# Winograd convolution with batch norm and SiLU: the first chunk's taps loaded in quarters between the x loads, and two matmuls on zeros ahead of the x tiles 2 to 14

## The chip, the cores and the metric

The kernel runs on one core of a Trainium2 chip. Time is device microseconds of that core; the median of three runs before the change is 193.27 us (192.41, 193.27 and 194.06). The engines are called by the profile's names: PE multiplies matrices (PEld loads its stationary operand), DVE and ACT are the vector and scalar engines, POOL is GpSimd, and SP issues nearly all transfers. Transfers run on 16 DMA engines, which share every load between them.

## The reference

The kernel computes a convolution over the sequence with three taps, then a batch norm with given statistics, then SiLU. The inputs are bfloat16.

```python
B, S, C = 2, 2048, 1024          # w is [3, C, C]
xp = jnp.pad(x, ((0, 0), (1, 1), (0, 0)))
y = sum(jnp.einsum('bsc,cd->bsd', xp[:, k:k + S, :], w[k]) for k in range(3))
y = (y - mean) * (g / jnp.sqrt(var + 1e-5)) + b
return jax.nn.silu(y)
```

## The kernel before, in words

The convolution is done by Winograd's method: six outputs of the sequence are made from eight inputs by eight products in place of eighteen. So there are three kinds of work.

**The x transform.** A batch's 2048 rows are cut into 17 windows of 126 rows (128 with the overlap), the last with 33. In this document w0 to w16 are the windows of batch 0 and w0' to w16' those of batch 1. `load_window` (L205 to L216) issues a window's load on SP: 128 rows of 2 KB, 256 KB in all. `transform` (L218 to L241) multiplies pieces of the window by a constant matrix `Rm` into PSUM (L225, 168 columns a matmul), and then one copy on ACT or DVE (L239, L241), chosen by a running cost, brings the group to `T_sb`. For batch 0 a window is two groups of four matmuls; each group has two PSUM banks, and the eight banks go round, so that a group reuses the banks of the group four before.

**The weight transform.** The output channels come in eight chunks of 128. A chunk's three taps are 256 KB each and are loaded as 1024 pieces of 256 bytes (`load_chunk`, L89). POOL makes six combinations of the taps from them, `uch` (`pair_sum` L163, `scale_weights` L149, `pair_tap` L173); the two other products use the raw taps 0 and 2. For chunk 0 POOL's order is: the sum of taps 0 and 2 (L163), tap 2 scaled, a second sum, tap 0 scaled, a third sum, then the first `uch` (L173), tap 1 scaled, and the five further `uch`.

**The units.** A unit is one chunk and one batch: eight products of eight matmuls each (`mms`, L250, 342 columns), and the output transform on ACT and DVE (L291, L298). The first unit (chunk 0, batch 0) takes product 7 first, which needs only the raw tap 2, and then 1, 3, 2, 4, 5, 0 and 6. Its matmuls are interleaved with the transform of batch 1: after each group of it a share of the first unit is run. From the second unit on there are only units, 64 matmuls each.

The order of each engine is the order in which the program is written (`manual_schedule`). On SP that means that a load that must wait holds back all that follow. There are two such waits. An x window's buffer is one of ten, so that a load waits until PE is done with the window ten before. And every load gets one of eight completion semaphores in turn, shared with the four parameter loads of the ACT queue: a load is issued only when the load eight before it has landed on all 16 engines.

The loop around the change, in the version before:

```python
for wi in range(NWIN):
    window = load_window(xpool, 0, wi)
    if wi in (3, 5, 13):
        load_chunk(0, {3: 0, 5: 2, 13: 1}[wi])
    for h in range(2):
        transform(0, wi, window, 4 * h, 4, (2 * wi + h) % 4 * 2, 2)
    if wi == 7: ...        # POOL: the sums of taps 0 and 2, with the scaling of taps 2 and 0
    if wi == 13: ...       # POOL: the six uch, with the scaling of tap 1
```

Seven matmuls on zeros (L203, 512 columns) stand ahead of everything on PE.

Of the kernel before, what the change touches and what calls it, by code (L numbers as in the profile page):

```python
# [32 lines left out]
NJ = 8  # L33
# [4 lines left out]
def kernel(  # L38
# [10 lines left out]
    nc = tc.nc  # L49
    B, S, C = x.shape  # L50
    D = w.shape[2]
    P = 128
    CT = C // P
# [19 lines left out]
    w_all = w.rearrange("k (ct p) d -> p k ct d", p=P)  # L73
    raw, wts, wx = {}, {}, {}
# [9 lines left out]
    def load_weights(dp):  # L84
        open_weights(dp)
        for k in (0, 2, 1):
            nc.sync.dma_start(out=pair_tile[dp][:, k], in_=w_all[:, k, :, dp * 2 * P:(dp + 1) * 2 * P])

    def load_chunk(dc, k):  # L89
        nc.sync.dma_start(out=raw[dc][k], in_=w_all[:, k, :, dc * P:(dc + 1) * P])  # L90

    open_weights(0)

# [15 lines left out]
    warm = consts.tile([P, 512], BF16, name="warm")  # L109
# [16 lines left out]
    for j in (0, 7):  # L126
        for k in range(NJ):
            if BT[j][k] != 0:
                nc.gpsimd.affine_select(
                    out=Rm[:, j, :],  # L130
                    in_=Rm[:, j, :],
# [12 lines left out]
    def scale_weights(dc, taps=(2, 1, 0), on_gpsimd=False):  # L144
        for k in taps:
            f = 2.0 if k == 1 else 4.0
            dst = wx[dc, k] = wtmp.tile([P, CT, P], BF16, name=f"w{k}x")
            if on_gpsimd:
                nc.gpsimd.tensor_scalar(dst, raw[dc][k], f, 0.0, op0=ALU.mult, op1=ALU.add)  # L149
            else:  # L150
                nc.scalar.mul(dst, raw[dc][k], f)

    def open_chunk(dc):
        wts[dc] = upool.tile([P, 6, CT, P], BF16, name="uch")
# [3 lines left out]
    def pair_sum(dc, n, engine=nc.gpsimd):  # L158

        e = outer[dc, n] = wtmp.tile([P, CT, P], FP32, name=("e1", "e2", "eh")[n])  # L160
        a = wx[dc, 0] if n == 2 else raw[dc][0]
        c = wx[dc, 2] if n == 1 else raw[dc][2]
        engine.tensor_tensor(e, a, c, op=ALU.add)  # L163
# [7 lines left out]
    def pair_tap(dc, n, op):  # L171
        odd = wx[dc, 1] if n else raw[dc][1]
        nc.gpsimd.tensor_tensor(wts[dc][:, 2 * n + (op == ALU.subtract)], outer[dc, n], odd, op=op)  # L173
# [14 lines left out]
    def turn_params():  # L188
        nc.tensor.transpose(prmT.rearrange("p q d -> p (q d)"), prm, ident[0:4 * DC, 0:4 * DC])
        nc.vector.tensor_scalar(rstd, prmT[:, 0, :], 1e-5, 1.0, op0=ALU.add, op1=ALU.mult)  # L190
        nc.gpsimd.tensor_tensor(rstd, rstd, mhalf, op=ALU.pow)

    def make_params():
        nc.vector.tensor_tensor(sc, prmT[:, 1, :], rstd, op=ALU.mult)
        nc.vector.tensor_tensor(beta, prmT[:, 2, :], sc, op=ALU.mult)
        nc.vector.tensor_tensor(beta, prmT[:, 3, :], beta, op=ALU.subtract)
        nc.vector.scalar_tensor_tensor(out=sk, in0=prmT[:, 1, :], scalar=C1, in1=rstd, op0=ALU.mult, op1=ALU.mult)
# [7 lines left out]
    def load_window(xpool, bi, wi):  # L205
        ntile = min(WT, NTB - WT * wi)
        t_lo = M_OUT * WT * wi - 1
        t_hi = min(t_lo + M_OUT * ntile + 1, S - 1)
        kk = t_hi - t_lo + 1
        if t_lo < 0:  # L210
            nc.sync.dma_start(out=xw0[1:113, :], in_=x[bi, 0:112, :])
            nc.sync.dma_start(out=xw0[113:kk, :], in_=x[bi, 112:t_hi + 1, :])
            return xw0, kk, ntile
        xw = xpool.tile([P, C], BF16, name="xw")
        nc.sync.dma_start(out=xw[0:kk, :], in_=x[bi, t_lo:t_hi + 1, :])  # L215
        return xw, kk, ntile  # L216

    def transform(bi, wi, window, ct0, n, bk, per):  # L218

        xw, kk, ntile = window  # L220
        width = 512 // per if per != 3 else 168
        banks = ps_all[:, bk * 512:(bk + (n + per - 1) // per) * 512]
        for c in range(n):
            at = (c // per) * 512 + (c % per) * width
            nc.tensor.matmul(  # L225
                banks[:, at:at + NJ * ntile],
                lhsT=xw[0:kk, (ct0 + c) * P:(ct0 + c + 1) * P],
                rhs=Rm[0:kk, :, 0:ntile],
                start=True,
                stop=True,  # L230
            )
        src = banks[:, 0:n * width].rearrange("p (s e) -> p s e", e=width)
        src = src[:, :, 0:NJ * ntile].rearrange("p s (j n) -> p s j n", j=NJ)
        dst = T_sb[bi][:, ct0:ct0 + n, :, WT * wi:WT * wi + ntile]
        cost = {e: f + m * n for e, (f, m) in EVAC.items()}
        eng = min(load, key=lambda e: load[e] + cost[e])
        load[eng] += cost[eng]
        if eng == "act":
            nc.scalar.copy(dst, src)  # L239
        else:  # L240
            nc.vector.tensor_copy(dst, src)  # L241
# [97 lines left out]
    def run(gen, n=None):  # L339
        while n is None or n > 0:  # L340
            if next(gen, run) is run:
                return
            if n is not None:
                n -= 1
# [3 lines left out]
    with tc.tile_pool(name="xwin", bufs=10) as xpool:  # L348
        for wi in range(NWIN):
            window = load_window(xpool, 0, wi)  # L350
            if wi in (3, 5, 13):
                load_chunk(0, {3: 0, 5: 2, 13: 1}[wi])
            for h in range(2):
                transform(0, wi, window, 4 * h, 4, (2 * wi + h) % 4 * 2, 2)
            if wi == 0:
                turn_params()
            if wi == 7:
                open_chunk(0)
                for n, taps in ((0, ()), (1, (2,)), (2, (0,))):
                    scale_weights(0, taps, on_gpsimd=True)  # L360
                    pair_sum(0, n)
            if wi == 13:
                pair_tap(0, 0, ALU.add)
                scale_weights(0, (1,), on_gpsimd=True)
                for n, op in ((1, ALU.add), (0, ALU.subtract), (1, ALU.subtract), (2, ALU.add), (2, ALU.subtract)):
                    pair_tap(0, n, op)
        make_params()
        first = unit(0, 0, 0, NTB, (0, 1, 2, 3), yTs[0], late, seven_first=True)
        load["act"] = load["dve"] = 0.0
        gi, done = 0, 0  # L370
        for wi in range(NWIN):
            window = load_window(xpool, 1, wi)
            if wi == 10:
                for k in (0, 2, 1):
                    load_chunk(1, k)
            for ct0, n in ((0, 3), (3, 3), (6, 2)):
                transform(1, wi, window, ct0, n, 4 + gi % 4, 3)
                gi += 1
                want = 52 * max(gi - 1, 0) // (3 * NWIN - 1)
                run(first, want - done)  # L380
                done = want
        load_weights(1)
        run(first)
# [68 lines left out]
    dc, bi = units[-1]  # L452
# [148 lines left out]
```

## Time and profile before

| what | before |
|---|---|
| median of 3 runs | 193.27 us |
| the profiled execution's own time | 193.53 us |
| its span, first to last instruction | 191.7 us |
| PE busy | 180.0 us (94%) |
| DVE busy | 161.3 us (84%) |
| POOL busy | 148.0 us (77%) |
| ACT busy | 122.6 us (64%) |
| mean granted clock of PE | 0.975 |
| moved by DMA | 31.72 MB |

The profile comes from one execution, and its times are microseconds from the first instruction. The 1.8 us between its span and its own time lie outside the instructions. A row of the timeline has the start, the length, the engine, the line, the operation and the tile (or tiles) that it writes and reads, and in brackets the idle time before it with what ended it. In a table of stretches each row has the busy time (and the number of instructions) of every engine in that stretch, then the clock that the throttle granted to PE (PEclk, 1.00 is full speed), the busy share of the DMA engines and the rate. Beside these views the trace keeps, for every load, sixteen completion counts, one for each DMA engine, with their times.

### The profile page before, as it was taken

The page shows a single profiled execution, that of the slowest core. Times are in us where ns is not written, and L with a number is a line of the kernel's source. Part 1 is how long each engine was busy: PE and PEld are TensorE (multiplying, and loading weights), DVE is VectorE, ACT ScalarE, POOL GpSimd, SP SyncE. Part 2 cuts the span into 40 slices and gives each one's busy share as a digit, 9 for nine tenths or more (in the row PEclk, how much of TensorE's full clock was granted, in tenths as well). Part 3 has the DMA queues.
Part 4 walks back from the last instruction along what each step waited for, and adds up shares of the span by engine and source line. Part 5 has one row for each costly group of instructions (what it writes and reads, how often), then busy time and mean ns, then how long its engine had stood idle before and what let it go on. Part 6 is the DMA issues. An engine that isn't in the chain of part 4 may idle for free.

```text
span 191.7 us, 3904 instructions
## 1 busy us (share of the span) xinstructions
PE 180.0 (94%) x1404; PEld 128.0 (67%) x1404; DVE 161.3 (84%) x347; ACT 122.6 (64%) x201; POOL 148.0 (77%) x89
## 2 busy tenths in 40 slices
PE   7579999999999999999999999999999999999960
PEld 3369688866666666666666666666666666669950
DVE  6557999987999699969996999699969987788981
ACT  3747878888287726873786287638755873635770
POOL 6359999999949996999699969996999699900000
PEclk9966999999999999999999999999999999999996
DMA  4999997990608387999292989783746465566425
GB/s 124 323 369 305 329 292 202 285 221 0 123 0 170 69 184 196 275 142 202 46 192 57 205 228 243 147 180 68 168 81 151 95 143 108 124 120 160 118 66 105
DMA packets 86759, 31.72 MB, mean 165 GB/s; under 512 B 73364, under 2 KB 82580, under 8 KB 86740
## 3 DMA queue, kind: packets, MB, share of 16 engines
q1 hardware_dynamic: 86637, 31.46, 70.1%
q8 instruction: 11, 0.18, 0.4%
q14 instruction: 8, 0.07, 0.1%
q10 hardware_dynamic: 103, 0.02, 0.0%
HBM read 14.82 MB, written 8.39 MB: 121 GB/s over the span
## 4 chain that ended last, share of the span: by engine, by line
PE 84%; DVE 6%; DMA 5%; ACT 2%; SPq 1%; issue 1%; DVEq 0%; ACTq 0%
PE ps_all L250 75%; PE ps_all L225 8%; DMA xw<-in_x_dram 5%; DVE T_sb L241 3%; ACT yT L261 1%; DVE y L487 1%; PE ps_all L465 1%; SPq L215 1%; DVE y L291 0%; SPq L90 0%; DVE d L487 0%; DVE ps_all L487 0%; DVE o_end L568 0%; ACT s L507 0%; ACT m L501 0%
## 5 line engine op out<-in xcount | busy, mean ns | idle before, releaser
L250 PE MATMUL ps_all<-T_sb,uch 128*128 128x342 bf16 (+2 forms) x816 | 123.0, 299 | 0.0
L250 PEld LDWEIGHTS <-uch 128*128 128x128 bf16 x816 | 77.0, 97 | 33.2 <-issue 0.2
L261 ACT ACTIVATE yT<-y,beta,sk 128x684 bf16<-128x684 f32 (+5 forms) x46 | 44.2, 960 | 30.3 <-DVE y L291 29.6
L250 PE MATMUL ps_all<-T_sb,wch 128*128 128x342 bf16 (+2 forms) x272 | 44.0, 300 | 0.2 <-DVE T_sb L241 0.2
L291 DVE SCALAR_TENSOR_TENSOR y<-ps_all,y 128x342 f32<-128x342 f32 x90 | 41.9, 507 | 1.7 <-PE ps_all L250 0.7
L173 POOL TENSOR_TENSOR uch<-e,wch 128x1024 bf16<-128x1024 f32 x16 | 33.8, 2134 | 10.8 <-PE ps_all L250 5.9
L173 POOL TENSOR_TENSOR uch<-e,w1x 128x1024 bf16<-128x1024 f32 x16 | 33.8, 2135 | 0.6
L225 PE MATMUL ps_all<-Rm,xw 128*128 128x168 bf16 (+1 forms) x272 | 31.2, 251 | 3.2 <-DMA xw<-in_x_dram 2.8
L173 POOL TENSOR_TENSOR uch<-eh,w1x 128x1024 bf16<-128x1024 f32 x16 | 33.8, 2132 | 0.6
L250 PEld LDWEIGHTS <-wch 128*128 128x128 bf16 x272 | 25.6, 97 | 11.5 <-DVE T_sb L241 0.4
L239 ACT CAST T_sb<-ps_all 128x672 bf16<-128x672 f32 (+5 forms) x45 | 26.3, 606 | 9.4 <-PE ps_all L225 8.3
L298 ACT COPY m<-ps_all 128x342 f32<-128x342 f32 x45 | 19.9, 442 | 19.0 <-PE ps_all L250 18.3
L241 DVE CAST T_sb<-ps_all 128x672 bf16<-128x672 f32 (+3 forms) x40 | 26.3, 698 | 5.6 <-PE ps_all L225 5.2
L225 PEld LDWEIGHTS <-xw 128*128 128x128 bf16 (+1 forms) x272 | 24.6, 106 | 8.5 <-DMA xw<-in_x_dram 3.5
L291 DVE SCALAR_TENSOR_TENSOR y<-ps_all,d 128x342 f32<-128x342 f32 x45 | 20.3, 507 | 0.5
L163 POOL TENSOR_TENSOR e<-wch,w2x 128x1024 f32<-128x1024 bf16 x8 | 17.0, 2130 | 0.2
L163 POOL TENSOR_TENSOR eh<-w0x,wch 128x1024 f32<-128x1024 bf16 x8 | 17.1, 2132 | 0.1
L291 DVE SCALAR_TENSOR_TENSOR y<-ps_all,s 128x342 f32<-128x342 f32 x30 | 14.0, 508 | 3.2 <-ACT s L298 3.2
L291 DVE SCALAR_TENSOR_TENSOR d<-m,ps_all 128x342 f32<-128x342 f32 x15 | 7.6, 507 | 9.3 <-ACT s L298 9.3
L291 DVE SCALAR_TENSOR_TENSOR ps_all<-m,ps_all 128x342 f32<-128x342 f32 x30 | 15.3, 509 | 0.0
L169 DVE TENSOR_REDUCE e<-wch 128x1024 f32<-128x2048 bf16 x6 | 13.7, 2277 | 0.0
L298 ACT COPY s<-ps_all 128x342 f32<-128x342 f32 x30 | 13.1, 438 | 0.0
(65 smaller groups left out, 83.4 us busy)
## 6 DMA issues: line engine op xcount, KB each, us to landing
xw<-in_x_dram SPq DMA_DIRECT2D x30, 256.0 KB
out_dram<-o_sb SPq DMA_DIRECT2D x30, 192.0 KB
wch<-in_w_dram SPq DMA_DIRECT2D x9, 512.0 KB
out_dram<-o_sb SPq DMA_DIRECT2D x15, 120.0 KB
wch<-in_w_dram SPq DMA_DIRECT2D x6, 256.0 KB
xw<-in_x_dram SPq DMA_DIRECT2D x2, 224.0 KB
out_dram<-o_sb SPq DMA_DIRECT2D x15, 7.5 KB
out_dram<-o_sb SPq DMA_DIRECT2D x15, 0.5 KB
```

The costliest lines, as they stand in the source:

```text
L163: engine.tensor_tensor(e, a, c, op=ALU.add)
L169: nc.vector.tensor_reduce(e, taps.rearrange("p k ct d -> p ct d k"), axis=mybir.AxisListType.X, op=ALU.add)
L173: nc.gpsimd.tensor_tensor(wts[dc][:, 2 * n + (op == ALU.subtract)], outer[dc, n], odd, op=op)
L215: nc.sync.dma_start(out=xw[0:kk, :], in_=x[bi, t_lo:t_hi + 1, :])
L225: nc.tensor.matmul(banks[:, at:at + NJ * ntile], lhsT=xw[0:kk, (ct0 + c) * P:(ct0 + c + 1) * P], rhs=Rm[0:kk, :, 0:ntile], start=True, sto ...
L239: nc.scalar.copy(dst, src)
L241: nc.vector.tensor_copy(dst, src)
L250: nc.tensor.matmul(ps_all[:, bk * 512:bk * 512 + c1 - c0], lhsT=lhsT, rhs=T_sb[bi][:, ct, j, c0:c1], start=start and ct == 0, stop=ct == C ...
L261: nc.scalar.activation(yT[:, i0:i1:step, c0:c1], y_all[:, i0:i1:step], ACT.Silu, bias=beta[:, dc:dc + 1], scale=sk[:, dc:dc + 1],)
L291: nc.vector.scalar_tensor_tensor(out=o, in0=i0, scalar=s, in1=i1, op0=ALU.mult, op1=op1)
L298: nc.scalar.copy(dst, src)
L465: nc.tensor.transpose(pv[0:n1 - n0, ENDS[k]], yT[:, k, n0:n1], ident)
```

## The change

Two things are changed in the loop over the windows of batch 0.

The three taps of chunk 0 are no longer loaded whole behind w3 (tap 0), w5 (tap 2) and w13 (tap 1). Each is loaded in four quarters of 64 KB, one quarter behind each of the x loads w1 to w12: tap 2 behind w1 to w4, tap 0 behind w5 to w8, tap 1 behind w9 to w12. POOL's sums are written after w8 where they were after w7.

Ahead of the first group of each of the windows w2 to w14 stand two matmuls on the zero tile `warm`, 168 columns each, into the first bank of that group, which the window's own matmuls then write over. There are 26 of them.

```diff
-    def load_chunk(dc, k):
-        nc.sync.dma_start(out=raw[dc][k], in_=w_all[:, k, :, dc * P:(dc + 1) * P])
+    def load_chunk(dc, k, c0=0, c1=CT):
+        nc.sync.dma_start(out=raw[dc][k][:, c0:c1], in_=w_all[:, k, c0:c1, dc * P:(dc + 1) * P])
...
-    def transform(bi, wi, window, ct0, n, bk, per):
+    def transform(bi, wi, window, ct0, n, bk, per, idle=0):
...
         banks = ps_all[:, bk * 512:(bk + (n + per - 1) // per) * 512]
+        for _ in range(idle):
+            nc.tensor.matmul(banks[:, 0:NJ * ntile], lhsT=warm[:, 0:P], rhs=warm[:, 0:NJ * ntile], start=True, stop=True)
...
-            if wi in (3, 5, 13):
-                load_chunk(0, {3: 0, 5: 2, 13: 1}[wi])
+            if 1 <= wi < 13:
+                tap, part = divmod(wi - 1, 4)
+                load_chunk(0, (2, 0, 1)[tap], part * CT // 4, (part + 1) * CT // 4)
             for h in range(2):
-                transform(0, wi, window, 4 * h, 4, (2 * wi + h) % 4 * 2, 2)
+                transform(0, wi, window, 4 * h, 4, (2 * wi + h) % 4 * 2, 2, idle=2 if 2 <= wi < 15 and h == 0 else 0)
             if wi == 0:
                 turn_params()
-            if wi == 7:
+            if wi == 8:
                 open_chunk(0)
```

## The prediction

> **What bounds the kernel now.** I read the chain that ended last first, then PE's timeline, the stretches with the clock, and at last who waits for which load.
>
> ```profile
> PE 84%; DVE 6%; DMA 5%; ACT 2%; SPq 1%; issue 1%; DVEq 0%; ACTq 0%
> PE ps_all L250 75%; PE ps_all L225 8%; DMA xw<-in_x_dram 5%; DVE T_sb L241 3%; ACT yT L261 1%; DVE y L487 1%; PE ps_all L465 1%; SPq L215 1%; DVE y L291 0%; SPq L90 0%; DVE d L487 0%; DVE ps_all L487 0%; DVE o_end L568 0%; ACT s L507 0%; ACT m L501 0%
> ```
>
> The units' matmuls (L250) are three quarters of the chain, and from 45 to 176 us PE is busy for 130.98 of 131.00 us. Whatever moves the start of that dense part moves the end by as much; the rest of the kernel cannot take it back or make it worse. So the question is what sets the start. PE's timeline up to there:
>
> ```profile
> 9.84 1.54 PE L225 MATMUL ps_all<-Rm,xw 128*128 128x168 bf16 x16 [1.84 <-DMA xw<-in_x_dram]
> 12.38 10.60 PE L225 MATMUL ps_all<-Rm,xw 128*128 128x168 bf16 x94 [1.01 <-DMA xw<-in_x_dram]
> 23.20 0.32 PE L250 MATMUL ps_all<-T_sb,wch 128*128 128x342 bf16 x1 [0.22 <-DVE T_sb L241]
> ```
>
> PE waits 1.84 us for w4 and 1.01 us for w6, and starts the first unit at 23.20. The stretches, cut where the clock changes (time, PE, PEld, DVE, ACT, POOL, clock, DMA, GB/s):
>
> ```profile
> 4.55:7.96 3.41, 2.68 (x32) 2.16 (x30) 1.78 (x4) 2.73 (x4) 1.66 (x1) 1.00 1.03 337
> 7.96:11.37 3.41, 1.55 (x17) 1.10 (x16) 1.81 (x4) 1.53 (x3) 0.00 (x0) 1.00 1.12 327
> 11.37:14.78 3.41, 2.40 (x19) 2.40 (x19) 1.47 (x2) 1.81 (x4) 2.91 (x2) 0.50 1.03 383
> 14.78:18.20 3.42, 3.42 (x27) 3.42 (x25) 2.58 (x4) 2.36 (x4) 3.27 (x3) 0.50 1.14 314
> 18.20:22.20 4.00, 3.82 (x46) 3.04 (x45) 4.00 (x6) 3.80 (x7) 3.92 (x3) 1.00 1.02 306
> ```
>
> PE runs at half clock from 11.37 to 18.20, after a stretch with 45% busy (1.55 of 3.41). A window takes 1.12 us there and some 0.74 us after it (w13 at 19.40, w14 at 20.16). But the DMA column is at 1.02 to 1.14 through all of it: the loads are saturated too. So I looked at when PE picks up the first windows of batch 1 (PEld rows):
>
> ```profile
> 23.43 0.10 PEld L250 LDWEIGHTS <-wch 128*128 128x128 bf16 x1
> 23.68 0.19 PEld L225 LDWEIGHTS <-xw 128*128 128x128 bf16 x3
> ```
>
> The second row is w1'. By the completion counts w1' has 15 of its 16 at 21.16 and the last at 23.63, 0.05 us ahead of its use. From 23.68 on PE is dense. **So two bounds meet here**: PE's own catching up (first unit at 23.20) and the landing of w1' (23.63). By the counts, the windows before are near as well: w14 lands at 19.58 and is used at 20.16, w15 at 20.41 and 20.93.
>
> **The change, part by part.**
>
> *Clock and dummies.* If the clock stayed full, PE would be done with batch 0 when the loads are. w16 lands at 20.87; PE finished it at 22.26. That is at most 1.4 us, but the program puts w0' and w1' next, with two matmuls of the unit between, and w1' lands at 23.63. What is late next is thus w1', and the gain on the path is 0.05 us, taken as nothing. It is the same if the clock does fall between 11 and 18 us. The 26 dummies take 0.073 us each (the pitch of w1's matmuls, 0.52 us for seven steps), 1.9 us in all, beside the waits for loads: a window with a quarter arrives every 0.95 us (below), its eight matmuls take 0.58 and the dummies 0.15. Without that cover they would cost up to 1.9 us.
>
> *Order of the loads.* In steady flow the last count of an x load comes 0.67 us after the one before (w6 12.33, w7 13.01, w8 13.67); tap 2 took 1.10 us (10.57 to 11.67), so a quarter is 0.28 us, an estimate, and a pair 0.95. w4 now has 0.75 of a tap ahead where it had a whole one: 0.28 us earlier. w6 has 1.25 for 2, w8 1.75 for 2; from w14 on all three taps are ahead in both orders. The bytes ahead of w1' are the same, so its landing stays at 23.63. Each load ends with a 4-byte packet of 9 to 14 ns on every DMA engine: nine more loads, **+0.1 us**.
>
> One 16 KB packet of instructions sits on one DMA engine from 20.97 for 1.08 us, and the step from w0'b (21.78) to w1' is 1.85 us. PE has 52 more instructions early (loads of weights included), so this packet may come earlier, ahead of w13. Then w14 to w16 are up to 1.1 us later, w16 at about 21.9 and PE done with it at 22.3, as before; w1' is still behind the same sum.
>
> *SP.* Its issues take 0.31 to 0.45 us each where not held back, 12 quarters for 3 taps: nine more, 4 us. They lie between issues that wait already:
>
> ```profile
> SPq L215 <- DMA xw<-in_x_dram: 3.1, 7, 0.7
> SPq L215 <- PE ps_all L225: 1.9, 6, 0.6
> ```
>
> (waits from 12 to 24 us: in all, times, longest). A pair needs some 0.85 us of SP for 0.95 us of transfer. Each load still waits for the one eight before, but eight are now four windows and four quarters, 3.8 us of transfer, where they were up to 5.4. The first load of all, with empty queues, took 2.76 us from issue to landing (0.72 to 3.48), so 3.8 us should still cover the round trip: cost nothing; its bounds are 0 and the lag rival's. Queued behind an SP wait are all later loads, so a lag here reaches w1'.
>
> The Trainium skill (DMA: Bandwidth & Descriptors, Rules for kernel authors) speaks against the quarters: it asks to coalesce small transfers, and holds those under 64 KB to be mostly overhead. Here a whole tap already takes 1.6 times as long as an x load of the same bytes (1.10 against 0.67), and both are one load: the row puts that on the 256-byte pieces, whose number does not change. By the rule the sum would be that of the lag rival below.
>
> *POOL.* Its first sum needs tap 2 and tap 0. Tap 2, the later one, lands at 11.67; now the last quarter lands behind w8: 13.67 less 0.28 (w8 has 1.75 taps ahead, not 2) plus 0.28, 13.67. POOL starts 2.0 us later, at 13.8, and its chain has no gap:
>
> ```profile
> 11.80 2.12 POOL L163 TENSOR_TENSOR e<-wch 128x1024 f32<-128x1024 bf16 x1 [3.87 <-DMA wch<-in_w_dram]
> ...
> 20.53 2.13 POOL L173 TENSOR_TENSOR uch<-e,wch 128x1024 bf16<-128x1024 f32 x1
> ...
> 23.76 2.13 POOL L173 TENSOR_TENSOR uch<-e,w1x 128x1024 bf16<-128x1024 f32 x1
> ```
>
> The `uch` for product 1 is ready at 22.66 and used at 25.94, that for product 3 at 25.89 and 28.62:
>
> ```profile
> 25.94 0.31 PE L250 MATMUL ps_all<-T_sb,uch 128*128 128x342 bf16 x1
> ...
> 28.62 0.31 PE L250 MATMUL ps_all<-T_sb,uch 128*128 128x342 bf16 x1
> ```
>
> The slack is 3.28 and 2.73 us; 2.0 of it is used up and 0.7 is left. It hides the delay as long as PE does not move; any gain over 0.7 us would end in a wait for POOL. Tap 1 was needed at 22.63 and lands near 17.5. Chunk 1's first `uch` has 11 us of slack.
>
> *Sum.* 0 (clock, w1' waits) + 0 (dummies, SP, POOL, under cover) + 0.1 (completions) = +0.1 us on the profiled 193.53 us, 193.6. That execution is 0.26 above the median of 193.27, so **193.4 us**, no change. For scale: 1%, 1.9 us, is about what a measurement of this kernel can tell from no change (the three runs span 1.65).
>
> **The rivals.**
>
> *Loads come earlier (gain), chance 0.2.* One DMA engine lags: tap 0's last count is 2.3 us after w3's (6.79, 9.11), its others 1.1. If that stall of 1.2 us belongs to the whole tap and goes, w1' lands 1.2 us earlier, and POOL's start is only 0.8 later, so its slack stays open. PE's bound allows that (22.26 less 1.4, and 0.9 to the first unit): up to -1.2, **192.2**. Against it: nothing of the kind happened at tap 2 or tap 1 (1.33).
>
> *The throttle falls into the dense part (slower), chance 0.12.* Dropping came with 45% busy, none with 79% (2.68 of 3.41). In the new rhythm PE is busy for 0.73 of 0.95, 77%; a stretch in which the instruction packet holds w13 back has about 0.73 * 2.3 / 0.95 = 1.8 of 3.41 us, 53%. It decides below a threshold that lies between 45 and 79. The half clock then begins near 21.6 (18.20 + 3.41) and lasts 3.4 or 6.8 us (before: 6.83, since 70% did not release it). From 23.2 on all of PE's time is on the path: half of 5.2 us, +2.6, **196.0**; half of 1.8, +0.9, if one stretch suffices. The Trainium skill (TensorE: Matmul & The Clock Gate, Why this matters for your kernels) says that the clock falls with idle gaps of some 3 us. By it this case has no chance, and the zeros no use. The trace differs: the longest gap ahead of the drop was 1.84 us.
>
> *The loads lag (slower), chance 0.13.* Eight in flight are too few, or a quarter costs more than a fourth of a tap. It decides from 0.95 us a pair on: nothing gives the time back, since the DMA engines are full behind w13 too. At 1.07 the nine pairs from w5 to w13 lose 1.1 us, all of it at w1': +1.1, **194.5**. At 1.2 they lose 2.2, 195.6; the last quarter of tap 0 is then at 14.6 (9.5 for w4, four pairs, 0.28), 2.9 later than tap 2 was, but PE is later still and POOL not in the way. At the far end a quarter takes as long as a tap, 1.10: twelve for three add 9.9 us, 203.3; I give that 0.01 of the 0.13.
>
> *The zeros don't keep the clock up.* Then it falls near 11.4 as before, and PE still catches up ahead of w1': the forecast's time, inside its chance of 0.55.
>
> **How the numbers follow.** Forecast 0.55 (192.7 to 194.0), gain 0.2, throttle 0.12, lag 0.13. Over 1% faster (under 191.3) is reached only if loads and POOL both come out better than worked out: 0.08. Over 1% slower (over 195.2): most of the throttle case and the tail of the lag, 0.15. Within: 0.77. The range runs from 192.1 (gain case whole) to 195.2, leaving the full throttle case and half of the outer tails out.
>
> **What would show it.** Right: PEld of w1' still starts at 23.4 to 24.0 and waits for its load; the first POOL sum at about 13.8; first L250 row near 23; PE dense after it; no wait of L250 for POOL. Wrong: w1' used ahead of 23, or a PEclk of 0.50 after 21 us, or PE waiting for `uch`.

## The result, and the profile after

| what | before | after |
|---|---|---|
| median of 22 runs each | 192.44 us | 194.26 us |
| lowest and highest of them | 191.47 to 195.43 | 192.97 to 196.56 |
| the profiled execution's own time | 193.53 us | 193.30 us |
| its span | 191.7 us | 191.5 us |
| mean granted clock of PE | 0.975 | 0.994 |

The ratio of the times is 1.009, with an interval of 1.0069 to 1.0112: the change makes the kernel slower by 0.9%, some 1.7 us. That is inside the range of the prediction (192.1 to 195.2) and inside 1%, but it is not "no change". The forecast was a shift of +0.1 us. That the time itself comes out only 0.9 us above the forecast of 193.4 is partly luck: the three runs on which it was built have a median of 193.27, the 22 of the same kernel 192.44.

The two profiled executions differ the other way, by 0.2 us, and that has to be cleared up first. One execution is one draw. The first profile of before lies 1.1 us above the median of its kernel, the profile of after 1.0 below its own. So nothing about the size of the loss is read from these two alone. One thing can be told from all runs: of the 22 of after, 14 have a mean granted clock of 0.99 or more, and their median is 193.8; the six such runs of before's second series (e10, below) have 192.30. So most of the loss, 1.5 us, is there with the clock up.

The first part of the chain that ended last, for the kernel after, by engine and then by line:

```profile
PE 81%; DMA 9%; DVE 4%; ACT 2%; SPq 1%; issue 1%; DVEq 0%; ACTq 0%
PE ps_all L255 75%; DMA xw<-in_x_dram 9%; PE ps_all L230 5%; DVE T_sb L246 1%; ACT yT L266 1%; DVE y L493 1%; PE ps_all L471 1%; SPq L90 1%; SPq L215 0%; DVE y L296 0%; DVE d L493 0%; DVE ps_all L493 0%; DVE o_end L574 0%; ACT s L513 0%; ACT m L507 0%
```

(L255 is L250 of before, L230 is L225, L246 is L241: the change adds five lines.) The units still have 75%. Loads of x have 9% of the chain where they had 5, and the transform's matmuls 5% where they had 8. So in these two profiles the chain runs through loads for 4% of the span more, and less through PE.

The stretches of the kernel after, cut where those of before were (time, PE, PEld, DVE, ACT, POOL, clock, DMA, GB/s):

```profile
4.55:7.96 3.41, 2.64 (x30) 2.14 (x29) 1.65 (x3) 2.60 (x4) 1.56 (x1) 1.00 0.91 287
7.96:11.37 3.41, 2.46 (x30) 1.97 (x29) 2.12 (x4) 1.78 (x3) 0.10 (x1) 1.00 0.96 289
11.37:14.78 3.41, 3.19 (x37) 2.45 (x36) 2.78 (x4) 2.89 (x4) 0.95 (x1) 1.00 1.09 316
14.78:18.20 3.42, 2.33 (x28) 1.72 (x25) 2.97 (x4) 2.23 (x3) 3.27 (x3) 1.00 1.04 325
```

The clock is full from 4.9 us to 189.2. But the last two columns of the first two rows are new: the DMA engines are at 0.91 and 0.96 with 287 and 289 GB/s, where they were at 1.03 and 1.12 with 337 and 327. **The loads are no longer saturated from 4.6 to 11 us**, though the bytes to be moved are the same.

The start of the dense part, and POOL:

```profile
22.95 0.10 PEld L255 LDWEIGHTS <-wch 128*128 128x128 bf16 x1 [0.30 <-DVE T_sb L246]
```

```profile
13.83 2.12 POOL L163 TENSOR_TENSOR e<-wch 128x1024 f32<-128x1024 bf16 x1 [5.76 <-DMA wch<-in_w_dram]
...
25.77 2.13 POOL L173 TENSOR_TENSOR uch<-e,w1x 128x1024 bf16<-128x1024 f32 x1
```

The first unit starts at 22.95. POOL starts at 13.83 (13.8 was predicted); product 3's `uch` is ready at 25.77 + 2.13 = 27.90 and used at 28.33, so 0.43 us of slack are left, and no unit matmul waits for POOL.

**From the start to the end.** The prediction said that the start of the dense part sets the end. It can be tested over all the profiles: an execution's own time less the time of its first unit matmul is 193.53 - 23.20 = 170.3 us for before and 193.30 - 22.95 = 170.35 for after, and 170.25 to 170.5 in four of the experiments below (e3, e1, e4 and e9: 192.02 - 21.77, 193.90 - 23.55, 193.87 - 23.40, 193.90 - 23.42). The second profile of after (e11), in which PE waits 0.6 us for ACT after its start, has 170.9; e8 and e7, in which it waits for POOL, have 170.9 and 171.3; and the five whose clock is at half in the dense part (e2, e5, e6, e10, e12) 171.3 to 172.8. So, as an estimate, the median of before stands for a start near 22.1, and that of after for one near 23.9. The question is what makes the loads of the first windows later by that much.

### The profile page after: what moved, and what is told of

The parts are those of the page before. It is cut to its first block, busy times and chain, and to the rows that moved or that the text cites. A ratio compares the mean times of both kernels' runs of the same rounds, so it can differ in the third digit from the quotient of the medians.

```text
span 191.5 us, 3968 instructions
## 1 busy us (share of the span) xinstructions
PE 180.2 (94%) x1430; PEld 126.7 (66%) x1430; DVE 162.0 (85%) x347; ACT 123.2 (64%) x201; POOL 148.0 (77%) x89
## 4 chain that ended last, share of the span: by engine, by line
PE 81%; DMA 9%; DVE 4%; ACT 2%; SPq 1%; issue 1%; DVEq 0%; ACTq 0%
PE ps_all L255 75%; DMA xw<-in_x_dram 9%; PE ps_all L230 5%; DVE T_sb L246 1%; ACT yT L266 1%; DVE y L493 1%; PE ps_all L471 1%; SPq L90 1%; SPq L215 0%; DVE y L296 0%; DVE d L493 0%; DVE ps_all L493 0%; DVE o_end L574 0%; ACT s L513 0%; ACT m L507 0%
## 5 line engine op out<-in xcount | busy, mean ns | idle before, releaser
L255 PE MATMUL ps_all<-T_sb,uch 128*128 128x342 bf16 (+2 forms) x816 | 123.1, 299 | 0.0
L255 PEld LDWEIGHTS <-uch 128*128 128x128 bf16 x816 | 76.9, 97 | 33.5 <-issue 0.2
L255 PE MATMUL ps_all<-T_sb,wch 128*128 128x342 bf16 (+2 forms) x272 | 44.0, 300 | 0.1
L255 PEld LDWEIGHTS <-wch 128*128 128x128 bf16 x272 | 25.6, 97 | 11.4 <-DVE T_sb L246 0.3
L230 PE MATMUL ps_all<-Rm,xw 128*128 128x168 bf16 (+1 forms) x272 | 29.6, 236 | 3.0 <-DMA xw<-in_x_dram 2.4
L246 DVE CAST T_sb<-ps_all 128x672 bf16<-128x672 f32 (+3 forms) x40 | 27.0, 700 | 4.6 <-PE ps_all L230 3.7
L230 PEld LDWEIGHTS <-xw 128*128 128x128 bf16 (+1 forms) x272 | 21.5, 98 | 9.4 <-DMA xw<-in_x_dram 5.6
```

Source lines behind the costliest of these rows:

```text
L230: nc.tensor.matmul(banks[:, at:at + NJ * ntile], lhsT=xw[0:kk, (ct0 + c) * P:(ct0 + c + 1) * P], rhs=Rm[0:kk, :, 0:ntile], start=True, sto ...
L255: nc.tensor.matmul(ps_all[:, bk * 512:bk * 512 + c1 - c0], lhsT=lhsT, rhs=T_sb[bi][:, ct, j, c0:c1], start=start and ct == 0, stop=ct == C ...
```

## The experiments

Three theories were open at first: the loads lag, because there are nine more of them; POOL's later start costs; the zeros cost.

### The parts of the change, one at a time

e1 is the change without the zeros:

```diff
-                transform(0, wi, window, 4 * h, 4, (2 * wi + h) % 4 * 2, 2, idle=2 if 2 <= wi < 15 and h == 0 else 0)
+                transform(0, wi, window, 4 * h, 4, (2 * wi + h) % 4 * 2, 2, idle=0)
```

> The quarters as in the change, without the 26 matmuls on zeros. POOL theory (POOL's chain starts 2 us later, and in the executions in which PE is earlier than in the profiled ones the first unit waits for uch): as slow as the change, 1.4 to 2.0 us over the kernel before; POOL's first sum at 13.5 to 14 us. Loads theory (24 loads in place of 15, SP and the eight in flight bring the x windows late): the same 1.4 to 2.0 us. Zeros theory (the 26 matmuls lie on PE's path, 0.073 us each): no difference from the kernel before, within 0.3 us.

e2 is the kernel before with the zeros alone: `transform` with `idle` as in the change, the taps whole behind w3, w5 and w13.

> The 26 matmuls on zeros, with the taps loaded whole behind w3, w5 and w13 as before. Zeros theory: 1.4 to 1.9 us slower than before. POOL theory and loads theory: no slower than before; a little faster (0 to 0.7 us) if keeping the clock up lets PE catch up ahead of w1'. The granted clock between 11 and 18 us is 1.00 if the zeros hold it.

e3 is the kernel before with tap 2 later, so that POOL starts late but no load is split:

```diff
-            if wi in (3, 5, 13):
-                load_chunk(0, {3: 0, 5: 2, 13: 1}[wi])
+            if wi in (3, 8, 13):
+                load_chunk(0, {3: 0, 8: 2, 13: 1}[wi])
...
-            if wi == 7:
+            if wi == 8:
```

> The taps whole, as many loads as before, no zeros; only tap 2 is loaded behind w8 in place of w5, and POOL's sums are written behind w8. That starts POOL as late as the change does (13.5 to 14 us) and leaves the rest. POOL theory: 1.4 to 2.0 us slower than before, like the change. Loads theory and zeros theory: within 0.3 us of before.

e4 splits the taps and moves nothing: POOL has its taps as early as before, and there are no zeros.

```diff
-                load_chunk(0, {3: 0, 5: 2, 13: 1}[wi])
+                for part in range(4):
+                    load_chunk(0, {3: 0, 5: 2, 13: 1}[wi], part * CT // 4, (part + 1) * CT // 4)
```

> Each tap in four quarters, but all four at the place of the whole tap (behind w3, w5 and w13), no zeros: as many loads as in the change, in the order of bytes of before, POOL's start near that of before (12 to 12.5 us). Loads theory: 1.4 to 2.0 us slower. POOL theory: at most 0.5 us slower. Zeros theory: within 0.3 us of before.

| kernel | loads of x and taps, batch 0 | median | ratio to before, interval |
|---|---|---|---|
| e1, quarters, no zeros | 30 | 194.85 | 1.0112 [1.0087, 1.0137] |
| e2, zeros alone | 21 | 192.96 | 1.0019 [0.9986, 1.0051] |
| e3, tap 2 late | 21 | 192.98 | 1.0006 [0.9972, 1.0041] |
| e4, quarters in place | 30 | 194.38 | 1.0095 [1.0065, 1.0124] |

(The first window is loaded in two parts, so 17 windows are 18 loads.) Two theories fall. The zeros cost nothing that can be measured (e2), and without them the change is as slow as with them (e1). POOL starts at 12.95 in e3, 1.15 us later than in before (13.5 to 14 was expected, so it tests a little over half of the change's delay), and the time is that of before; in e4 it starts at 11.31, earlier than in before, and the time is that of the change. What all the slow kernels have, and no other, is the taps in quarters.

### Is it the split, or the number of loads?

e5 leaves the taps whole and adds nine loads that move next to nothing, 16 pieces of 4 bytes, into a small tile that nothing reads:

```diff
+    bits = consts.tile([P, 9, 2], BF16, name="bits")
...
+            elif 1 <= wi < 13 and wi != 12:
+                i = (1, 2, 4, 6, 7, 8, 9, 10, 11).index(wi)
+                nc.sync.dma_start(out=bits[0:16, i], in_=x[0, 0:16, 2 * i:2 * i + 2])
```

> The kernel before with nine more loads on SP that move nothing to speak of (16 pieces of 4 bytes, into a tile that is not read), behind w1, w2, w4 and w6 to w11, so that as many loads are issued on SP and take one of the eight semaphores as in the change; taps whole, no zeros. Issue theory (SP's 0.45 us for each further load and its place among the eight in flight take SP's lead, and the DMA engines run dry): 1.0 to 2.0 us slower than before, DMA busy share under 0.9 in stretches between 5 and 10 us. Split theory (a tap cut in quarters is dearer to transfer): within 0.3 us of before.

It took 196.28 us (6 runs), a ratio of 1.0172 [1.0126, 1.0219]: 3.3 us for 576 bytes, more than the 1.0 to 2.0 expected. So a loss at least as large comes without any split: it is that there are more loads. In its profile w15 lands at 22.60, and at 19.5 to 20.7 in the four with whole taps and no added loads (before, e10, e2, e3). Not all of the 3.3 us is the loads' own, though. All six runs have a mean granted clock of 0.966 to 0.982; in the profile the clock is at half from 21.0 to 27.8 us, and the time less the start of the first unit is 171.3, 0.9 more than with the clock up.

e6 goes half way, six halves of 128 KB, tap 2 behind w2 and w4, tap 0 behind w6 and w8, tap 1 behind w10 and w12, no zeros, POOL's sums after w8. That is three loads more than before, not nine.

```diff
-            if wi in (3, 5, 13):
-                load_chunk(0, {3: 0, 5: 2, 13: 1}[wi])
+            if 2 <= wi < 13 and wi % 2 == 0:
+                tap, part = divmod(wi // 2 - 1, 2)
+                load_chunk(0, (2, 0, 1)[tap], part * CT // 2, (part + 1) * CT // 2)
```

> Taps in halves, one behind each of w2, w4 and so on to w12: three more loads than before in place of nine, interleaved as in the change; no zeros. Issue theory: two windows and a half take SP 1.4 us for 1.9 us of transfer, so that SP keeps its lead: at most 0.6 us slower than before. A theory by which the interleaving itself is dear (short and long pieces in turn): 1.0 to 2.0 us slower, as e1.

192.62 us, a ratio of 0.9994 [0.9961, 1.0027]: the time of before. Three more loads cost nothing, nine cost 1.7 us; where between them the cost begins was not tried. The table of stretches shows the difference. The same 5 us of seven profiles, in this order: before, before again (e10, below), e6, after, after again (e11, below), e1, e4. Columns as above; the last two are the DMA share and the rate.

```profile
5.00:10.00 5.00, 2.44 (x30) 1.99 (x29) 2.55 (x4) 3.36 (x5) 1.66 (x1) 1.00 1.08 317
```

```profile
5.00:10.00 5.00, 3.96 (x38) 3.14 (x37) 2.99 (x5) 3.41 (x6) 1.66 (x1) 1.00 1.04 299
```

```profile
5.00:10.00 5.00, 3.57 (x37) 2.62 (x35) 2.99 (x5) 3.65 (x6) 1.66 (x1) 1.00 1.07 323
```

```profile
5.00:10.00 5.00, 3.88 (x45) 2.97 (x42) 3.37 (x5) 4.02 (x6) 1.66 (x1) 1.00 0.87 270
```

```profile
5.00:10.00 5.00, 4.15 (x45) 3.50 (x43) 3.38 (x5) 4.17 (x6) 1.66 (x1) 1.00 0.92 270
```

```profile
5.00:10.00 5.00, 3.08 (x35) 2.32 (x33) 3.39 (x5) 3.85 (x6) 1.66 (x1) 1.00 0.92 266
```

```profile
5.00:10.00 5.00, 3.23 (x37) 2.52 (x35) 2.61 (x5) 3.49 (x5) 1.66 (x1) 1.00 1.01 272
```

With 21 or 24 loads the DMA engines are full (1.04 to 1.08, 299 to 323 GB/s). With 30, the quarters one by one from w1 on, they run dry: 0.87 to 0.92 and 266 to 270 GB/s. In e4, whose eight quarters of these 5 us stand together, the rate is as low (272) at a share of 1.01, and the share falls to 0.93 from 10 to 15. (In e5 it is 1.02 from 5 to 10 and 0.87 from 10 to 15, later than was expected.) Against the 317 of the first profile, the 270 of after over 5 us are 0.24 MB less, nine tenths of an x window, which takes 0.67 us in steady flow; against the 299 of e10 they are 0.15 MB, 0.4 us. So this stretch makes up 0.4 to 0.6 us of the loss, and not all of it.

The completion counts show the same in another way. From its issue to its first count w4 takes 4.07 us in before, 3.62 in e10 and 3.58 in e6, but 2.67 in after, 2.73 in e11, 2.87 in e1 and 2.56 in e4; the first load of all, with nothing ahead of it, takes 2.37 in after. So with quarters w4 finds next to no queue ahead of it at the DMA engines, and otherwise one of a microsecond or more.

### Why they run dry: SP's pace, or eight in flight

Two things can hold the loads back, and both are in the traces. SP's queue in the kernel after (start, length, line):

```profile
5.94 0.47 SPq L215 DMA_DIRECT2D xw<-in_x_dram  x1
6.45 0.43 SPq L90 DMA_DIRECT2D wch<-in_w_dram  x1
6.93 0.47 SPq L215 DMA_DIRECT2D xw<-in_x_dram  x1
7.44 0.43 SPq L90 DMA_DIRECT2D wch<-in_w_dram  x1
7.91 0.47 SPq L215 DMA_DIRECT2D xw<-in_x_dram  x1
```

There is no wait between these issues. A window and its quarter take 0.47 + 0.43 us, and with the steps between them a pair goes out every 0.98 us (5.94, 6.93, 7.91), where the DMA engines could move a pair in 0.95. The chain of the second profile of after (e11) goes through them, one behind the other:

```profile
0.72 2.75 DMA xw<-in_x_dram
3.49 0.37 SPq L90
...
7.86 0.47 SPq L215
8.37 0.43 SPq L90
8.85 4.30 DMA xw<-in_x_dram
13.19 0.75 PE ps_all L230 x8
...
14.17 5.38 DMA xw<-in_x_dram
19.60 0.77 PE ps_all L230 x8
20.39 2.28 DVE T_sb L246 x3
```

SP stands until w0 has landed (0.72 + 2.75 = 3.47), and then the chain is nothing but issuing up to 8.85. The same place in e3, with whole taps:

```profile
5.45 0.43 SPq L215
5.92 0.43 SPq L215
6.39 0.43 SPq L215
6.87 0.44 SPq L90
7.36 6.13 DMA xw<-in_x_dram
```

Here an issue every 0.47 us stands for a window, 0.67 us of transfer, so SP gains 0.2 us on the DMA engines with each, and a queue builds up ahead of them. With pairs it gains nothing, and no queue is built. In e4 it loses: four quarters, 1.1 us of transfer, take SP 1.93 and 1.97 us, with no wait.

```profile
3.54 1.93 SPq L90 DMA_DIRECT2D wch<-in_w_dram  x4
...
6.50 1.97 SPq L90 DMA_DIRECT2D wch<-in_w_dram  x4
```

The other limit, eight in flight, takes over in the kernel after from 10.57 on. There an x load is issued just as the load eight before it lands: w9 at 10.57 with w5 landed at 10.56, w10 at 11.53 with w6 at 11.51, w11 at 12.55 with w7 at 12.47. In that stretch the windows w5 to w10 land 0.93 to 0.97 us apart, the pace of the transfer, and the DMA engines are full again:

```profile
10.00:15.00 5.00, 4.18 (x48) 3.36 (x49) 3.40 (x5) 3.30 (x6) 1.17 (x1) 1.00 1.08 317
```

But the lag grows on behind it. With e10 as the measure, w8 of after has 1.75 taps ahead of it for 2 and yet lands at 13.40 for 12.93, which makes it 0.75 us late (a quarter taken as 0.28); w14, with three taps ahead in both, lands at 19.96 for 18.53, 1.4 us late. In e11 the two are 0.5 and 1.8. So a quarter to a half of the lag has arisen by w8, and most of the rest from w9 to w13, whose loads SP issues with waits again. These are differences of single executions.

Two kernels were made to weigh the one against the other. In e9 the quarters start only behind w4 (no zeros), so that the first issues are clear of them.

```diff
-            if wi in (3, 5, 13):
-                load_chunk(0, {3: 0, 5: 2, 13: 1}[wi])
+            for q in {4: (0, 1), 5: (2, 3), 6: (4, 5), 7: (6,), 8: (7,), 9: (8,), 10: (9,), 11: (10,), 12: (11,)}.get(wi, ()):
+                tap, part = divmod(q, 4)
+                load_chunk(0, (2, 0, 1)[tap], part * CT // 4, (part + 1) * CT // 4)
```

> As many loads as e1 (12 quarters, no zeros), but the first quarters come behind w4: two behind each of w4, w5 and w6, then one behind each of w7 to w12, tap 1 whole in its quarters behind w9 to w12 as in the change. SP issues w1 to w4 with nothing between. If the loss of e1 is made in the first 10 us, where SP's issues stand back to back and the DMA engines run dry behind them: between 0.3 and 1.2 us slower than before, and less slow than e1 (which was 2.2). If every further load costs by itself, or the eight in flight do from w9 on: as e1, 1.8 to 2.4 us.

194.12 us, 1.0091 [1.006, 1.0121]. That is hardly better than e1 (1.0112), the intervals overlap, and it lies between the two outcomes that were expected. The dry stretch came later. In the rows of e9 and of e3 from 10 to 15 us

```profile
10.00:15.00 5.00, 3.39 (x31) 2.86 (x32) 2.96 (x4) 3.02 (x5) 1.49 (x1) 0.83 0.96 302
```

```profile
10.00:15.00 5.00, 4.00 (x48) 3.17 (x46) 4.07 (x6) 4.09 (x7) 2.05 (x1) 1.00 1.10 349
```

it moves 302 GB/s for 349. Its SP issues without a wait from 7.94 to 11.41, again a pair every 0.98 us. So e9 moved SP's limit and did not remove it; as a test it tells less than was meant.

e12 puts the nine tiny loads behind w8 to w16, where SP had gained a lead.

```diff
+    bits = consts.tile([P, 9, 2], BF16, name="bits")
...
+            if 8 <= wi < 17:
+                i = wi - 8
+                nc.sync.dma_start(out=bits[0:16, i], in_=x[0, 0:16, 2 * i:2 * i + 2])
```

> The nine loads of 16 pieces of 4 bytes again, in the kernel before, but behind w8 to w16 in place of w1 to w11. There SP has the first eight windows issued and waits between its issues anyway, so that their issue time is nearly covered; but of eight loads in flight only four are then windows, 2.7 us of transfer. If the early issues are what costs (SP has no lead, the DMA engines run dry): at most 0.6 us slower than before. If the eight in flight are what costs: 1.0 to 2.5 us slower, with the DMA busy share under 0.9 between 12 and 20 us.

195.92 us (6 runs), 1.0176 [1.0135, 1.0218], as much as the early ones and more than the 1.0 to 2.5 us expected. Here too the clock takes a part: all six runs have a mean granted clock of 0.973 to 0.985, and in the profile it is at half from 22.3 to 25.7. That profile starts its first unit at 23.53, as late as e1 (23.55), and its time less the start is 171.65, 1.3 more than with the clock up. Its stretches:

```profile
10.00:15.00 5.00, 3.90 (x47) 3.23 (x45) 3.89 (x6) 3.93 (x7) 3.94 (x3) 1.00 0.89 308
15.00:20.00 5.00, 2.43 (x27) 1.67 (x24) 3.58 (x5) 2.72 (x4) 4.85 (x4) 1.00 0.82 218
20.00:24.00 4.00, 3.18 (x33) 2.60 (x34) 2.59 (x8) 2.24 (x4) 3.92 (x3) 0.78 0.76 228
```

Here it is the other limit. The loads issued at 10.79, 11.53, 12.14 and 12.88 go out 0.01 to 0.08 us after the load eight before them has landed (10.77, 11.45, 12.13, 12.81). With every second load empty, eight in flight are four windows, 4 * 0.67 = 2.7 us of transfer, and a load takes 2.75 us from issue to landing with empty queues. So the DMA engines run dry under each limit: eight in flight where only 2.7 us of transfer are in flight (e12), SP's pace where quarters are issued back to back (after, e11, e9, e4). For the change itself the traces point to SP for the part of the lag up to w8, since in that stretch SP never waits; for the later part they do not. Neither limit was tried by itself (the quarters issued from another engine's queue would do that for SP), so **how the 1.7 us are shared between the two is not measured**.

### Can the gain be had without the extra loads?

The profile of before suggested that w14 to w16 come too late, behind tap 1. e7 and e8 load tap 1 whole behind w1' instead, with POOL's six `uch` written after that; e7 has the zeros, e8 not.

```diff
-            if wi in (3, 5, 13):
-                load_chunk(0, {3: 0, 5: 2, 13: 1}[wi])
+            if wi in (3, 5):
+                load_chunk(0, {3: 0, 5: 2}[wi])
...
+            if wi == 1:                      # windows of batch 1
+                load_chunk(0, 1)
+                pair_tap(0, 0, ALU.add)      # and the rest of what stood at wi == 13
```

> An attempt at a faster version: taps 0 and 2 whole behind w3 and w5 as before, tap 1 behind w1' in place of w13, with the products of tap 1 written there; with the 26 matmuls on zeros. If the landing of w1' sets the start of the dense part, it comes 1.1 us earlier, and the landing of w2' (unchanged) leaves some 0.3 us of that: 0.2 to 0.6 us faster than before. If PE's catching up is the bound, no difference.

> The same without the zeros. If the landing of w1' sets the start of the dense part: 0.2 to 0.6 us faster, where PE's clock allows it. If PE's catching up is the bound: no difference. If tap 1 is too late for POOL (its first uch then needs it at about 20.5 and gets it at 22): slower by up to 0.5 us.

e7 took 192.27 us, 0.998 [0.995, 1.001]; e8 took 192.49, 0.9979 [0.9949, 1.0009]. Neither is shown to be faster. The profile of e7 says why. Its first unit starts at 20.81, 0.96 us ahead of that of e3 (21.77). But at the 121st unit matmul the two are level, 49.42 and 49.40. In between PE waits for POOL, and POOL for tap 1 (who waits for whom from 20 to 60 us: in all, times, longest):

```profile
POOL uch L173 <- DMA wch<-in_w_dram: 1.7, 1, 1.7
PEld L255 <- POOL uch L173: 0.9, 2, 0.6
...
PE ps_all L255 <- POOL uch L173: 0.4, 1, 0.4
```

So the earlier start ends in a wait for POOL. But POOL's own wait of 1.7 us is for tap 1, which these two kernels load later; the wait for POOL that the prediction had for gains over 0.7 us, with tap 1 early, was not tested.

### Both kernels again

To see how much one profile differs from the next, both kernels were run once more, beside e9.

> The kernel before, unchanged, for a second profile. If the profile on which the prediction rests was an execution in which the loads came late: w1' lands near 22 us in place of 23.63, no DMA engine lags by 1.2 us from tap 0 on, and the profiled execution takes some 1 us less than the 193.53 of the first.

> The changed kernel, unchanged, for a second profile. Issue theory: SP's issues without a wait between from 3.5 to 10 us, about 0.98 us a pair, DMA busy share under 0.9 in stretches there, w1' landing at 23.3 to 24.3 us, and the start of the dense part 1 to 2 us later than in the second profile of before.

Before took 192.58 us, 0.9996 [0.9963, 1.0028] to itself; after took 193.77, 1.0065 [1.0036, 1.0093]. The loss of the change was thus measured at 0.9 and 0.65%, and without its zeros at 1.1%. The profile of e10 took 195.52 us, not 1 us less than the first as expected, with the clock at half in the dense part (below); its loads of batch 0, which had landed before that, can be read, and so they were above. As expected, w1' lands near 22 (22.23), and no DMA engine lags by 1.2 us after tap 0 (w4's last two counts are at 8.92 and 9.11). In e11 w1' lands at 22.77 for the 23.3 to 24.3 expected, and the first unit starts at 23.14, 0.4 us behind that of e10 (22.70) where 1 to 2 was expected. So these two profiles differ by less than the medians do.

## Why the prediction was right and wrong, point by point

**The start sets the end: right, with the clock up and no wait for POOL.** Time less start is 170.25 to 170.5 us in six profiles, from 192.02 to 193.90, and 170.9 to 171.3 in the three in which PE waits once more behind it; with a half clock in the dense part it is 171.3 to 172.8.

**The clock and the dummies: right in the sum.** The clock stayed full in after, and nothing was gained by it. But e1 and e3, without zeros, kept the full clock through the first 45 us too, so that the zeros held it up is not shown; in e2, with zeros, it fell at 22.2. They cost nothing (e2).

**POOL: right.** Start 13.83 for 13.8, slack 0.43 for 0.7, no wait of a unit for POOL in after, and no cost in e3.

**SP: this step failed.** The sentence is "A pair needs some 0.85 us of SP for 0.95 us of transfer", and with it "cost nothing". The 0.85 is about two issues of the lengths read (0.31 to 0.45), with no steps between them. In the kernel after, a window's issue behind a quarter takes 0.47, a quarter's 0.43, and the two steps some 0.04 each: a pair needs 0.98, more than its transfer. So the cover of a tenth of a microsecond was not there, and the issues did not "lie between issues that wait already": in the kernel after SP doesn't wait once from 3.97 to 9.84. The change as a whole costs 1.2 to 1.8 us (after, e11: 194.26 and 193.77 against 192.44 and 192.58); what part of it is this step stays open. The other half of the step, eight in flight with 3.8 us of transfer "cost nothing", held only in part: in after the pace of 0.95 a pair was kept from w5 to w10, and then three pairs, w10 to w13, took 3.74 us for 2.85.

**The outcome was on the list, under another cause.** "The loads lag (slower), chance 0.13" has the place (all of it ahead of the dense part), the point of decision ("from 0.95 a pair on") and a price: 194.5, 0.24 above the measured 194.26. That nearness is luck: as a shift it is +1.1 us on a base of 193.4, and 1.7 was measured on 192.44. Of its two conditions, "eight in flight are too few, or a quarter costs more than a fourth of a tap", the second is not what the trace of after shows: the quarters of w5 to w10 land 0.20 to 0.21 us behind their windows, less than the 0.28 estimated. The first is not shown for the lag up to w8, and is open for the part behind it. At least the first part of the lag was in the step that had been costed at nothing. The loss also isn't spread over nine pairs: it sits in single steps, 1.83 us from w4 to w5 and 1.77 from w11 to w12 where a pair takes 0.95. The second step has one part that the prediction named: a 16 KB packet of instructions, at 20.97 in the first profile of before, stands at 15.51 for 0.96 us in after (15.47 and 1.16 in e11), and w12's last count comes 0.7 us behind its fifteenth in both. In the kernels with whole taps that packet also comes before w16 has landed (18.59 in e10, 17.71 in e3), so it doesn't explain the loss by itself. Why the first step is there isn't settled.

**"Two bounds meet" held for one profile only.** In the first profile of before w1' had its last count at 23.63, 2.47 us after the one before: one DMA engine had run some 1.3 us behind the others since tap 0. In other executions with whole taps w1' lands at 22.23 (e10), 22.13 (e2) and 21.77 (e3); in after at 22.60 (used 23.40) and in e11 at 22.77 (used 23.60). So w1' is not the bound, and the sign named for it, w1' waiting for its load, is not there. What bounds the start, as far as the rows show, are the last windows of batch 0 with their copies. Take w15: with whole taps it lands at 19.51 (e3), 20.05 (e10), 20.41 (before) and 20.68 (e2), on average 20.2; with quarters at 20.93 (after), 21.12 (e11), and 21.39, 21.40 and 21.40 (e4, e1, e9), on average 21.2. (With halves, e6, it is 21.04, but that profile is of an execution of 194.86 us, 2.2 above its kernel's median.) The difference of 1.1 us is one of single executions; the medians of before and after say 1.8. PE's rows in the second profile of after show the wait, 0.75 us for w12 and 0.33 for w13:

```profile
18.37 0.75 PE L230 MATMUL ps_all<-Rm,xw 128*128 128x168 bf16 x8 [0.75 <-DMA xw<-in_x_dram]
19.60 0.75 PE L230 MATMUL ps_all<-Rm,xw 128*128 128x168 bf16 x8 [0.33 <-DMA xw<-in_x_dram]
```

From w13 on its chain (above) goes through the copies, 2.28 us of DVE, to the first unit at 23.14.

**The Trainium skill's rule.** The Trainium skill (DMA: Bandwidth & Descriptors, Rules for kernel authors) asks to coalesce small transfers and counts those under 64 KB as mostly overhead. The advice held here, though the quarters, of 64 KB, lie just at that size: 12 of them cost 0.9% where 3 loads of 256 KB did not. But the price did not go with the size of a load. Nine loads of 64 bytes cost 1.7% (a part of it by the clock), though they take the DMA engines hardly any time: w7 and w8 of e5 land 0.65 us apart with one between them. Halves cost nothing. In these runs the number of loads decides, against SP's pace and against eight in flight. Another page of the Trainium skill (Perfetto Trace Analysis, DMA Optimizations) says that splitting may let some transfers start sooner, and helps where the DMA engines are generally idle. They were at 1.03 to 1.12 here, so its condition was not met, and e4, e1 and after agree with that.

## What to carry to other kernels

Where transfers are the limit, count loads as well as bytes. Compare the issuing engine's pitch, issued back to back, with the transfer time of what it issues, and the transfer time of all that may be in flight with the round trip of one load; the pitch is the distance from start to start, not the length of an issue, and the margin of a tenth of a microsecond was no cover here. Before a sum is made on one profile, see whether that execution lies near the median, because what bounds a late one (here one lagging DMA engine) need not bound the kernel. And forecast a shift against the median of many runs: here three runs gave a base 0.8 us too high.

## What the runs showed of the hardware that was not expected

**Empty loads can cost as much as full ones.** With nine loads of 64 bytes the kernel takes 3.3 us longer, early (e5) or late (e12); in their two profiles 0.9 and 1.3 us of the excess lie behind the start, with the clock at half. What such a load takes is hardly transfer time but an issue of 0.31 to 0.47 us on SP and one of eight places in flight. Whether such loads also lower the clock, whose mean is 0.966 to 0.985 in all twelve runs, is not shown.

**The clock can fall in the dense part, in the kernel before too.** It was at half in five of fourteen profiles there or just ahead of it: e2 (22.2 to 25.6), e5 (21.0 to 27.8), e6 (23.4 to 26.8), e10 (20.9 to 27.7) and e12 (22.3 to 25.7), with zeros and without. In four more it fell earlier (11.4 to 18.2 in before, and 3.4 us long between 11.3 and 16.7 in e4, e8 and e9), and in five not at all ahead of the end (after, e11, e1, e3, e7). The stretches of e10:

```profile
17.50:20.90 3.40, 1.65 (x22) 1.22 (x21) 1.99 (x4) 1.44 (x3) 3.32 (x3) 0.99 1.06 247
20.90:24.30 3.40, 2.74 (x23) 2.23 (x22) 2.35 (x8) 1.71 (x4) 3.32 (x3) 0.50 1.04 377
24.30:27.70 3.40, 3.40 (x21) 2.73 (x20) 1.79 (x3) 1.43 (x3) 3.40 (x3) 0.50 1.11 340
```

Two stretches at half clock, and the execution took 195.52 us, 2.9 above the median of its runs. Its time less its start is 172.8, 2.5 more than with the clock up. That is the prediction's second rival with its price (+2.6), in the kernel before. It did not come from the change: the profiles of after and e11 do not have it.

**The busy share of a stretch did not decide it.** The clock fell after stretches of 3.4 us with PE busy for 45% (before), 49% (e10, above) and 59%, and stayed up after 51% and 53% (e1, 18.2 to 21.7). The 59% and the 51% are both from e2, the kernel with zeros:

```profile
8.50:11.90 3.40, 1.72 (x20) 1.42 (x20) 2.00 (x3) 1.91 (x3) 0.29 (x1) 1.00 1.10 332
...
18.80:22.20 3.40, 2.02 (x27) 1.65 (x28) 2.03 (x3) 1.71 (x3) 3.40 (x2) 1.00 1.03 294
22.20:25.60 3.40, 3.40 (x22) 2.58 (x20) 2.33 (x9) 1.66 (x3) 3.32 (x3) 0.50 1.00 324
```

(2.02 of 3.40 is 59%, and the next stretch is at 0.50.) So the threshold between 45 and 79% that the prediction looked for is not one in this view; what does decide stays open. The Trainium skill (TensorE: Matmul & The Clock Gate, Why this matters for your kernels) names idle gaps of some 3 us. In the first profile of before the longest gap ahead of the fall was 1.84 us, and in e10 the longest in the 3.4 us ahead of it 0.99, so the traces differ from the rule in its size.
